# Sixteen of 28 quarter sums of the output weights moved from batch 1 to the end of the first stretch, in a fused cross attention and SwiGLU kernel

## The chip, the cores and the metric

The kernel runs on one core of a Trainium2 chip. The metric is the device time of the whole kernel in microseconds, the median of repeated executions. A profiled execution, recorded separately, gives the traces that are read here; its *span* reaches from the first to the last recorded instruction, and its own device time is a little longer. The engines are written as the profile writes them: PE is TensorE (matrix products), PEld its loads of stationary operands, DVE is VectorE, ACT is ScalarE, POOL is GpSimd, and SP is SyncE, whose queue issues most of the DMA transfers.

## The reference

Two parts follow each other. The first is a block recurrent cross attention: for each of 8 batches and 8 heads, 512 tokens `x` attend to 32 state vectors, and the state vectors attend to the tokens, with 64 elements per head:

```python
scores = scale * np.matmul(x, state.transpose(0, 1, 3, 2))
a = softmax(scores);  xread = np.matmul(a, state)
a2 = softmax(scale * np.matmul(state, x.transpose(0, 1, 3, 2)))
sread = np.matmul(a2, x)
attn = np.concatenate([xread, sread], axis=2)
```

(`softmax` stands for the maximum, exponential and division that the reference writes out.) The heads are joined into rows of 512, 544 rows per batch, 4352 in all. The second part is a feed-forward net on these rows: an RMS norm, two products with weights 512 x 1536 (`w_gate`, `w_val`), `silu(g) * val`, and a product with `w_out`, 1536 x 512. Its weights arrive as 64-bit floats.

## The kernel before, in words

**Stages.** The core works through a first stretch, then batches 1 to 7, then the state rows of all batches together. Each stage is a set of generators, called streams. Each stream yields after a step of one or a few instructions. A string of letters, one letter per step, deals the steps of the streams in order; with the schedule set to manual, that is the order of each engine's instructions. `ORDER` deals the first stretch, `FIRST` batch 1, `PERIOD` batches 2 to 6, `LAST` batch 7 and `STATES` the state rows. An engine executes its own steps in the order in which the letters come; between engines only data and buffers are waited for.

**The first stretch** (404 letters before). It converts the weights: `exponents` (letter e, on ScalarE, lines 234 to 239) and `values` (d, on VectorE, lines 260 to 272) turn each piece of raw 64-bit numbers into 32-bit floats `w_m` (first layer, one tile per pair `mp` of hidden blocks) and `wo` (output weights). It reads the tokens and the states of batches 0 and 1 (a, A and s, S: transposes, scores, softmax; lines 289 to 526, line 289 on GpSimd). It multiplies the first-layer weights of a pair with the states (`own_weights`, v, the product at L567), so that the hidden layer of batch 0 needs only products with the attention weights: letters h (products, L610), t (silu, L616) and u (VectorE's product, L620). The output projection of batch 0 follows as hidden blocks become ready (`project_as_ready`, p, L817), and c copies and stores it. Letter w begins batch 1 (`slot_sums` and its first two pairs of `own_weights`, with `more_of_v`, L594 to L597, on GpSimd). Letter k is `weight_sums` (L860): twelve VectorE instructions that make differences of the halves of the output weights, three tiles t1, t2 and t4 and one difference in place, in three rounds of four, one instruction per step. Letter z, 42 times, is `keep_awake`, a product that nothing uses.

**Batches 1 to 7** compute the hidden layer and the projection with two forms of fast matrix multiplication that save products and cost sums. In `hidden_seven` seven block products (L714, letter h) serve for eight, with ScalarE's copies (t) and VectorE's sums at lines 777 to 802 (u). In `project_twice` seven products of halves (letter p, L1017) are each split once more into seven products of quarters. The left-hand sums are made by VectorE (`quarter_sums` and `half_sums`, L1065 to L1076, letter k), the results are joined by VectorE at L1057 and by GpSimd at L1043 to L1048. Meanwhile the next batch's tokens and states are read (a, s), its `own_weights` made (v, w, x), and SP loads inputs (l), fetches first-layer weights (f, L187) and stores results (o).

**The quarter sums of the output weights.** Each of the seven outer products of `project_twice` needs three sums of quarters of its output weights, and one difference in place. `weight_quarters` (L965 to L974, letter q) makes them once, on GpSimd: seven groups of four instructions at L971, 28 in all. The groups come in the order of `outer_weights`: two blocks of the output weights, then t2, t1, two more blocks (one of them holds the difference in place), t4. After the fourth instruction of a group SP stores its three sums to DRAM (`t2_d`, L973). Every batch, batch 1 too, fetches them back one group at a time (`fetch_quarters`, L963): letters G are the first three fetches of batch 1, letters g always fetch three groups ahead. All these tiles come from one pool of three, `quarters_w`, opened with the other late pools by `open_late` at the first letter c, k or w of the first stretch.

Of the kernel before, what the change touches and what calls it, by code (L numbers as in the profile page):

```python
# [19 lines left out]
W_BUFS = 3  # L20

ORDER = (
    "zzzzzzzzzzazadaaaaaaaaazzzdzzzzzzeaeeaaaaadaadeeaaaaeeezdeazdzzzzzzadeeeaadaadzz"
    "zzzzzzzaaaaaddadzzzzvvvaaedzaAAdaaassdAAAAaAAeeAaAhtddddehehhuppedddddvtduppeeee"
    "ddvvdddeeeedAAddhhtuhhpeAddeApAtddeesvuvddveApdddhheedtupddeeehtAAAddhueeeddsApA"
    "AAdpepvvevAsddddedddphtsssseeehuhAdtssddpdshuedeedpvvvAeApdeAehtdhhAueddppAdddtA"
    "eeddpAheuSSAAAeAAvAvvpehhtSSddhdAAASSpAtuSShSSSdkAuwwsSSSpcpcskpwckkkkkkkkpwkkwc"
    "wwww"
)

PERIOD = (
# [4 lines left out]
)  # L36

FIRST = (
    "vhththhhthfhhuuuhtttuqqqqaxxaaauhthhhvquuhuxqxxaavtuhhththhfaxthhhqqquuuuxxtuhut"
    "hthhthhuaakaavfuuxhtuuhutthqqfhhutxxuqqqqqqhauthuuxhhaautthaaasshtuuhuuthuGhskuk"  # L40
    "GuGukkppqqpppqpppugqqpkkkklkppqpppkcpcqgaakppgqqkskaakaaaaqqppkkpppkppkkpkpkpkpa"
    "cosaaaacgpapgaskkkkkkaosaapppppgcppppcaappaskkakkapppkpapkappaakpookkoosaassfsww"
    "xssswxlscxxcoxofxg"
)
LAST = (
    "vxhhffththhtuhhhavuttuuhhtfuhhgxxthhhuuuxxtuthuhtthuhuxhutuvxxxvhthhutkxghhtuhut"
# [11 lines left out]
def kernel(  # L58
# [791 lines left out]
    def weight_sums():  # L850

        t1, t2, t4 = (seven["t"][:, i] for i in range(3))
        for k in range(0, HM, 2):
            def blk(i, j):
                return wo[:, HM * i + k:HM * i + k + 2, HD * j:HD * j + HD]
            for dst, a, b in ((t1[:, k:k + 2], blk(0, 1), blk(0, 0)),
                              (t2[:, k:k + 2], blk(1, 1), t1[:, k:k + 2]),
                              (blk(0, 1), blk(1, 1), blk(0, 1)),
                              (t4[:, k:k + 2], blk(1, 0), t2[:, k:k + 2])):
                VE.tensor_tensor(out=dst, in0=a, in1=b, op=ALU.subtract)  # L860
                yield
# [272 lines left out]
    done = object()  # L1134
# [18 lines left out]
    def first_of_batch(b):  # L1153
        slot_sums(b)
        yield
        for mp in range(2):
            for part in own_weights(b, mp):
                yield from part
# [12 lines left out]
    for k in range(1, RAW_AHEAD):  # L1171
# [5 lines left out]
               "v": (step for mp in range(NM // 2) for part in own_weights(0, mp) for step in part),  # L1177
               "h": of_batch_0(0), "t": of_batch_0(1), "u": of_batch_0(2),
               "p": project_as_ready(banks_0), "c": projected(banks_0, store_tokens(0)),
               "w": first_of_batch(1), "k": weight_sums(), "z": keep_awake()}  # L1180
    by_hand = dict(engines={mybir.EngineType.PE, mybir.EngineType.DVE,
                            mybir.EngineType.Activation, mybir.EngineType.Pool,
                            mybir.EngineType.SP})
    with tc.manual_schedule(**by_hand):
        for stream in ORDER:
            if stream in "ckw" and "s" not in seven:
                early.close()
                open_late()
            next(streams[stream])
        assert all(next(stream, done) is done for name, stream in streams.items() if name != "z")  # L1190

        for b in range(1, B):
            h, t, u = hidden_seven(S, weights_of(b), lambda b=b: tokens_of(b), True)
            p, c, k, o = project_twice(b, store_tokens(b))
            own = [own_weights(b, mp) for mp in range(2, NM // 2)]
            then = [own_weights(b + 1, mp) for mp in range(2)] if b + 1 < B else []
            streams = {"h": h, "t": t, "u": u, "p": p, "c": c, "k": k,
                       "v": (step for part in own for step in part[0]),
                       "x": (step for part in own + then for step in part[1])}
            streams.update(o=o, f=fetches(b), g=fetches_of_quarters(b))  # L1200
            if b == 1:
                streams.update(q=weight_quarters(), G=first_fetches_of_quarters())
            if b + 1 < B:
                streams.update(l=loads(b + 2) if b + 2 < B else iter((0, 0)), a=tokens_read(b + 1), s=states_read(b + 1),
                               w=first_products(b + 1, then))
            else:
                streams["a"] = (step for part in (state_norm(), sums_of_w([0])) for step in part)
            for stream in FIRST if b == 1 else LAST if b + 1 == B else PERIOD:
                next(streams[stream])
            assert all(next(stream, done) is done for stream in streams.values())  # L1210
        n = B * (NM // 2)
        h, t, u = hidden_seven(NT, (state_weights, state_sums), state_tokens, True,
                               lambda mp: fetch(n + mp + W_BUFS))
        p, c, k = project_seven(NT, store_states, nc.scalar)
        list(weights_back())
        streams = {"h": h, "t": t, "u": u, "p": p, "c": c, "k": k, "y": sums_of_w(range(1, NM // 2))}
        for stream in STATES:
            next(streams[stream])
        assert all(next(stream, done) is done for stream in streams.values())
# [29 lines left out]
```

## Time and profile before

Three executions took 764.33, 761.76 and 761.35 us: the median is 761.76 us.

| what | value |
|---|---|
| median | 761.76 us |
| profiled execution, own time | 762.78 us |
| its span | 760.5 us |
| instructions | 14354 |
| TensorE busy | 747.2 us, 98% |
| VectorE busy | 600.3 us, 79% |
| ScalarE busy | 351.1 us, 46% |
| GpSimd busy | 294.0 us, 39% |
| first stretch, to the last product L567 | 135.78 us |
| batch 1 | 87.64 us |
| batches 2 and 3 | 80.19 and 80.16 us |
| quarter sums L971 in batch 1 | 28, 31.48 us of GpSimd |

The busy time of an engine counts its recorded instructions, and an average over the span mixes stages with different limits; so the borders of the stages were taken from the timeline of TensorE (the last product of each stage), and busy times read between them. A line of a group or of the timeline names the source line, the engine, the operation, the written tile `<-` the read tiles, the shape, and how many instructions are meant; what stands in brackets is the idle time before it and what ended it. "Pair 5" below is the last pair of hidden blocks. In the timeline one product of the code is two records.

### The profile page before, as it was taken

Reading aid. Unit: us, or ns where it says so; the run is one execution under the profiler, and the core shown is the slowest. Engines: PE = TensorE matmul, PEld = TensorE weight load, DVE = VectorE, ACT = ScalarE, POOL = GpSimd, SP = SyncE. Lnnn points to the kernel's source line nnn. Section 1 sums busy time; section 2 is a strip of 40 time slices with the busy share of each in tenths; the row PEclk is TensorE's granted clock in tenths of the full one; section 3 lists DMA queues with packets and bytes.
Section 4 is the critical chain, followed back from the end, with each engine's and each line's share of the span. In section 5 each row is a group of like instructions: output and inputs, shape, how many; then the busy total and the mean of one; then the engine's idle time right before and its main releaser. Section 6 shows DMA issues by size and latency. Waiting matters only on the chain.

```text
span 760.5 us, 14354 instructions
## 1 busy us (share of the span) xinstructions
PE 747.2 (98%) x5608; PEld 595.3 (78%) x5608; DVE 600.3 (79%) x1000; ACT 351.1 (46%) x548; POOL 294.0 (39%) x379
## 2 busy tenths in 40 slices
PE   8899999999899999999999999999999999999998
PEld 6534435678778798879877997889788987899997
DVE  3999997679956898589947994799579975787961
ACT  4898974553225532654155424553355236411220
POOL 2000002893675325542374038312843266323700
PEclk9999999999999999999999999999999999999999
DMA  9787754695576266834774376617662756133411
GB/s 291 214 277 264 289 214 162 231 305 178 195 234 242 56 244 214 297 78 181 256 245 151 125 267 219 222 40 306 217 228 39 293 184 241 56 90 119 140 56 28
DMA packets 61890, 146.15 MB, mean 192 GB/s; under 512 B 15744, under 2 KB 32640, under 8 KB 54912
## 3 DMA queue, kind: packets, MB, share of 16 engines
q1 hardware_dynamic: 48704, 125.78, 47.3%
q10 hardware_dynamic: 13120, 19.47, 9.0%
q8 instruction: 44, 0.72, 0.4%
q14 instruction: 22, 0.18, 0.1%
HBM read 116.46 MB, written 28.77 MB: 191 GB/s over the span
## 4 chain that ended last, share of the span: by engine, by line
PE 88%; DVE 8%; POOL 1%; ACT 1%; issue 1%; DMA 0%; SPq 0%; ACTq 0%; POOLq 0%; DVEq 0%
PE f L714 36%; PE f L1017 27%; PE f L817 6%; PE pv L610 5%; PE at L567 3%; PE pv L567 2%; PE f L880 2%; PE at L345 1%; PE f L1149 1%; PE at L509 1%; PE at L440 1%; DVE hb L1076 1%; DMA out_dram<-kept 0%; PE at L296 0%; DVE hb L790 0%
## 5 line engine op out<-in xcount | busy, mean ns | idle before, releaser
L714 PE MATMUL f<-aT_s,v 128*128 128x256 f32 x504 | 119.6, 382 | 0.0
L714 PEld LDWEIGHTS f<-aT_s,v 128*128 128x128 f32 x504 | 94.5, 190 | 24.8 <-issue 9.2
L777 DVE TENSOR_TENSOR g<-g,f 128x512 f32<-128x512 f32 x84 | 57.3, 685 | 42.6 <-PE f L714 38.6
L1043 POOL TENSOR_TENSOR kept<-kept 128x256 f32<-128x256 f32 x28 | 23.1, 826 | 175.0 <-DVE kept L1057 173.6
L714 PE MATMUL f<-aT_t,vs 128*128 128x256 f32 x336 | 87.2, 383 | 0.3 <-ACT g L761 0.3
L1027 ACT COPY kept<-f 128x512 f32<-128x512 f32 (+1 forms) x56 | 29.7, 532 | 124.8 <-PE f L1017 83.0
L1017 PE MATMUL f<-w,h 128*128 128x128 f32 x588 | 74.6, 276 | 1.0 <-DVE h L1067 1.0
L714 PEld LDWEIGHTS f<-aT_t,vs 128*128 128x128 f32 x336 | 62.4, 190 | 16.0 <-POOL vs L594 4.2
L1017 PEld LDWEIGHTS f<-w,h 128*128 128x128 f32 x588 | 69.6, 192 | 5.4 <-issue 4.1
L768 ACT ACTIVATE hb<-g 128x1024 f32<-128x1024 f32 x42 | 44.5, 1058 | 56.7 <-DVE g L777 56.6
L594 POOL TENSOR_TENSOR vs<-v 128x256 f32<-128x256 f32 x42 | 31.7, 755 | 80.4 <-ACT v L579 80.4
L289 POOL TENSOR_TENSOR ri<-ss,mhalf 128x4 f32<-128x4 f32 x8 | 10.4, 1295 | 124.5 <-DVE ss L371 114.6
L766 ACT COPY g<-f 128x512 f32<-128x512 f32 x42 | 24.6, 586 | 44.5 <-PE f L714 44.5
L714 PE MATMUL f<-aT_t,v 128*128 128x256 f32 x168 | 43.5, 381 | 1.6 <-DVE c L777 1.6
L817 PE MATMUL f<-wo,hb 128*128 128x512 f32 x96 | 44.4, 600 | 0.0
L610 PE MATMUL pv<-aT_s,v 128*128 128x512 f32 x96 | 43.7, 597 | 0.3 <-ACT t L616 0.3
L714 PE MATMUL f<-aT_s,vs 128*128 128x256 f32 x168 | 43.6, 382 | 0.0
L790 DVE TENSOR_TENSOR hb<-hb,c 128x512 f32<-128x512 f32 (+1 forms) x48 | 36.9, 768 | 8.0 <-ACT hb L768 7.3
L790 DVE TENSOR_TENSOR hb<-hb,f 128x512 f32<-128x512 f32 (+1 forms) x48 | 31.0, 646 | 15.0 <-PE f L714 15.0
L1017 PE MATMUL f<-wo,h 128*128 128x128 f32 x336 | 42.2, 275 | 0.0
L1017 PE MATMUL f<-wo,hb 128*128 128x128 f32 x336 | 42.1, 275 | 0.0
L777 DVE TENSOR_TENSOR c<-c,f 128x512 f32<-128x512 f32 (+1 forms) x48 | 31.2, 650 | 12.6 <-PE f L714 12.5
(183 smaller groups left out, 1689.1 us busy)
## 6 DMA issues: line engine op xcount, KB each, us to landing
w_m<-w_d SPq DMA_DIRECT2D x48, 1024.0 KB, 5.9
w<-t_d SPq DMA_DIRECT2D x49, 576.0 KB, 5.4
out_dram<-kept SPq DMA_DIRECT2D x56, 128.0 KB, 2.1
raw<-in_moe_w_val_dram SPq DMA_DIRECT2D x6, 1024.0 KB, 5.5
raw<-in_moe_w_out_dram SPq DMA_DIRECT2D x6, 1024.0 KB, 7.1
w_d<-w_m SPq DMA_DIRECT2D x6, 1024.0 KB, 4.9
x_b<-in_x_dram SPq DMA_DIRECT2D x6, 1024.0 KB, 7.5
x_d<-xB ACTq DMA_DIRECT2D x6, 1024.0 KB, 4.2
```

Of the source, the lines that this page charges most:

```text
L567: TE.matmul(out=pv[e][Ns * j:Ns * j + Ns, :], lhsT=stT_g[b][D * e:D * e + D, j, :], rhs=w[D * e:D * e + D, j].rearrange("p m k f -> p (m k ...
L594: GE.tensor_tensor(out=vs[:, 0], in0=a21, in1=a22, op=ALU.add)
L610: TE.matmul(out=to[0], lhsT=lhs(i, k), rhs=r, start=(i == 0), stop=(i == len(rhs) - 1))
L714: TE.matmul(out=ps[:, i, 0:half], lhsT=l[:, i, :], rhs=r, start=(start and i == 0 and k == 0), stop=(k == len(lhs) - 1), skip_group_check= ...
L766: SE.copy(gates(q)[1], q["x"][:, :, 0:half])
L768: SE.activation(out=hb[:, 2 * mp:2 * mp + 2, 0:n].rearrange("p m (c t) -> p m c t", c=2), in_=q["g"][:, :, :, 0:half], func=ACTF.Silu if s ...
L777: VE.tensor_tensor(out=to, in0=to, in1=q[ps][:, :, 0:half], op=ALU.add)
L790: VE.tensor_tensor(out=part, in0=part, in1=val, op=ALU.mult)
L817: TE.matmul(out=banks[r], lhsT=hb[:, m, P * r:P * r + P], rhs=wo[:, m, :], start=(m == 0), stop=(m == NM - 1))
L1017: TE.matmul(out=to[half][:, slot, :], lhsT=lhs[:, k, :], rhs=rhs[:, k, :], start=(fresh and n in (0, 4) and k == 0), stop=(k == QM - 1), s ...
L1027: SE.copy(k[:, 4 * i:4 * i + 4 - i], banks[name][i])
L1043: GE.tensor_tensor(out=k[:, 1:3], in0=k[:, 0:1].to_broadcast([P, 2, QD]), in1=k[:, 1:3], op=ALU.add)
```

## The change

Sixteen letters q are added to `ORDER`, among its last letters, which then has 420; `FIRST` has 12 in place of 28, and 322 letters in place of 338. The generator `weight_quarters` is made with the first stretch's streams and handed on to batch 1. All other letters occur as often as before in each string, and in another order. The other four stages' strings are the same. From line 1181 on the line numbers of the kernel after are higher by one.

```diff
--- before.py
+++ after.py
@@ -20,12 +20,12 @@
 W_BUFS = 3
 
 ORDER = (
-    "zzzzzzzzzzazadaaaaaaaaazzzdzzzzzzeaeeaaaaadaadeeaaaaeeezdeazdzzzzzzadeeeaadaadzz"
-    "zzzzzzzaaaaaddadzzzzvvvaaedzaAAdaaassdAAAAaAAeeAaAhtddddehehhuppedddddvtduppeeee"
-    "ddvvdddeeeedAAddhhtuhhpeAddeApAtddeesvuvddveApdddhheedtupddeeehtAAAddhueeeddsApA"
-    "AAdpepvvevAsddddedddphtsssseeehuhAdtssddpdshuedeedpvvvAeApdeAehtdhhAueddppAdddtA"
-    "eeddpAheuSSAAAeAAvAvvpehhtSSddhdAAASSpAtuSShSSSdkAuwwsSSSpcpcskpwckkkkkkkkpwkkwc"
-    "wwww"
+    "zzzzzzzzzzaazdaaaaaaaaadeeaazzezzzzzzzzzzzzzzazzaaaaadadzzzzaaazzeeeeedadzadaadz"
+    "zadaaazzeeeedzdzaaaadvAaavdadaAAaavessaAAAeAeAAdahhhhteeeddddddtuppdddvdAAeeeupv"
+    "ddvhhhheeeeddAdtAAeddpdeAupteedsddvedAddeepvvhhheeeAddtupdAeetAeepdAdduppdAAdAdv"
+    "vhdvhAdeAduheeddAsssddAsdppsdtuhedeeedApdtdAedAsedhuddvpvvhhethssduepeeedtseAApp"
+    "AAAddddAddAveeepvhddsvAAdhhhhkAqsuASttSSSqkukqkkqquAAwpqSSSSwSwwwwwkkpkSSSpcqpkp"
+    "SSkckkqqqqcpcqqqqwwq"
 )
 
 PERIOD = (
@@ -36,11 +36,11 @@
 )
 
 FIRST = (
-    "vhththhhthfhhuuuhtttuqqqqaxxaaauhthhhvquuhuxqxxaavtuhhththhfaxthhhqqquuuuxxtuhut"
-    "hthhthhuaakaavfuuxhtuuhutthqqfhhutxxuqqqqqqhauthuuxhhaautthaaasshtuuhuuthuGhskuk"
-    "GuGukkppqqpppqpppugqqpkkkklkppqpppkcpcqgaakppgqqkskaakaaaaqqppkkpppkppkkpkpkpkpa"
-    "cosaaaacgpapgaskkkkkkaosaapppppgcppppcaappaskkakkapppkpapkappaakpookkoosaassfsww"
-    "xssswxlscxxcoxofxg"
+    "qhhtaahGtathhuvvhhulhxxttfaatuhhtaaxxxuuxhuqqqqhhuuththhhththaaaahuuhuuuhtttffGh"
+    "uuhtvxxxqkkvxkkhuhuhuxaathtahutuhhtahhuuxuuthhtuhthhtaahhuauGuuuuhpptaaqfugaaupa"
+    "hqpuuuppgqkkkkckkakpqappgkkkcppppkppkkkkakkkssspppcpppcpppppcpppppaakassaaosskkk"
+    "aokaaaaackakkpkqapppkppppppppqgkpakgoossaalkssaakkksoosppcsaapwwwxxxxxppcfgxoofs"
+    "sg"
 )
 LAST = (
     "vxhhffththhtuhhhavuttuuhhtfuhhgxxthhhuuuxxtuthuhtthuhuxhutuvxxxvhthhutkxghhtuhut"
@@ -1177,7 +1177,8 @@
                "v": (step for mp in range(NM // 2) for part in own_weights(0, mp) for step in part),
                "h": of_batch_0(0), "t": of_batch_0(1), "u": of_batch_0(2),
                "p": project_as_ready(banks_0), "c": projected(banks_0, store_tokens(0)),
-               "w": first_of_batch(1), "k": weight_sums(), "z": keep_awake()}
+               "w": first_of_batch(1), "k": weight_sums(), "q": weight_quarters(), "z": keep_awake()}
+    quarters_made = streams["q"]
     by_hand = dict(engines={mybir.EngineType.PE, mybir.EngineType.DVE,
                             mybir.EngineType.Activation, mybir.EngineType.Pool,
                             mybir.EngineType.SP})
@@ -1187,7 +1188,7 @@
                 early.close()
                 open_late()
             next(streams[stream])
-        assert all(next(stream, done) is done for name, stream in streams.items() if name != "z")
+        assert all(next(stream, done) is done for name, stream in streams.items() if name not in "qz")
 
         for b in range(1, B):
             h, t, u = hidden_seven(S, weights_of(b), lambda b=b: tokens_of(b), True)
@@ -1199,7 +1200,7 @@
                        "x": (step for part in own + then for step in part[1])}
             streams.update(o=o, f=fetches(b), g=fetches_of_quarters(b))
             if b == 1:
-                streams.update(q=weight_quarters(), G=first_fetches_of_quarters())
+                streams.update(q=quarters_made, G=first_fetches_of_quarters())
             if b + 1 < B:
                 streams.update(l=loads(b + 2) if b + 2 < B else iter((0, 0)), a=tokens_read(b + 1), s=states_read(b + 1),
                                w=first_products(b + 1, then))
```

## The prediction

> **What bounds the kernel now.** I read the busy shares first, then the busy time by stage, then the waits of TensorE in each stage, then the timelines of VectorE and GpSimd side by side.
>
> ```profile
> PE 747.2 (98%) x5608; PEld 595.3 (78%) x5608; DVE 600.3 (79%) x1000; ACT 351.1 (46%) x548; POOL 294.0 (39%) x379
> ```
>
> TensorE (PE) sets the time; only 13.3 of its 760.5 us are idle, so a gain can come only from idle or stretched TensorE time. The table by stage says where that is (borders at the last product of each stage; columns: length, then busy time and instructions of each engine):
>
> ```profile
> core 0: us, PE busy (x) PEld busy (x) DVE busy (x) ACT busy (x) POOL busy (x), PEclk, DMA share, GB/s
> 0.00:40.31 40.31, 35.60 (x187) 24.62 (x187) 28.51 (x46) 26.90 (x37) 6.00 (x28) 1.00 0.87 249
> 40.31:112.96 72.65, 72.65 (x329) 29.59 (x329) 69.64 (x87) 63.22 (x74) 0.00 (x0) 1.00 0.73 260
> 112.96:135.78 22.82, 22.82 (x166) 11.16 (x166) 18.56 (x32) 11.79 (x19) 5.16 (x7) 1.00 0.56 201
> 135.78:223.42 87.64, 83.27 (x671) 68.20 (x663) 71.19 (x116) 33.13 (x56) 61.99 (x67) 1.00 0.67 219
> 223.42:303.61 80.19, 80.19 (x670) 68.21 (x662) 64.44 (x115) 35.54 (x59) 35.54 (x47) 1.00 0.57 197
> ```
>
> The first stretch ends at 135.78. Batch 1 takes 87.64, batch 2, with the same products, 80.19 (batch 3: 80.16): batch 1 has 7.45 us too many, 4.37 of them idle TensorE. It differs by GpSimd's 28 quarter sums (L971, 31.48 us) and 6.8 us more busy VectorE (DVE) for one more instruction. TensorE's waits in batch 1; batch 2 shows none:
>
> ```profile
> PE f L714 <- DVE c L777: 1.6, 1, 1.6
> PE at L440 <- DVE aT_s L433: 1.0, 1, 1.0
> PE f L1017 <- DVE h L1067: 1.0, 1, 1.0
> PE at L524 <- DVE sr L520: 0.7, 1, 0.7
> ```
>
> All four name VectorE. The timelines (start, duration) say why; the second and fourth line are GpSimd's at the same moments:
>
> ```profile
> 143.35 1.21 DVE L790 TENSOR_TENSOR hb<-hb,c 128x512 f32<-128x512 f32 x1 [0.26 <-ACT hb L768]
> ...
> 143.97 1.45 POOL L971 TENSOR_TENSOR wo<-wo 128x384 f32<-128x384 f32 x1
> ...
> 193.37 2.93 DVE L1076 TENSOR_TENSOR hb<-hb 128x768 f32<-128x768 f32 x2
> ...
> 193.77 1.72 POOL L971 TENSOR_TENSOR wo<-wo 128x384 f32<-128x384 f32 x1
> ```
>
> L790 takes 0.69 elsewhere, L1076 0.95 each, L971 1.01 alone: on overlap both stretch. Divided over all, 6.8/28 = 0.24 us of VectorE per quarter sum.
>
> [...] L790 and L1076 (two SBUF inputs) are stretched by 0.5 to 0.8 us, L777 (one input in PSUM) keeps 672 to 689 ns throughout.[...]
>
> **The change, part by part.** No arithmetic is added or removed. 16 of 28 letters q move from batch 1's string into the last part of the first stretch's, and both strings are dealt anew, which permutes products, copies and sums of these two stages on every engine.[...] I worked from the built order of each engine, with durations from the trace of before (for queued instructions the spacing of starts).
>
> *1. The first stretch gets longer.* Up to the conversion that starts at 36.14 both orders hold equal VectorE work. From there before's VectorE is the near-critical engine: 69.64 of 72.65 us busy. Its last piece of the weights of pair 5, which a TensorE product (L567) needs, ends at 111.2:
>
> ```profile
> 109.97 1.22 DVE L272 SCALAR_TENSOR_TENSOR w_m<-raw,ex 128x1024 f32<-128x1024 f32 x1
> ...
> 111.94 1.09 PE L567 MATMUL at<-w_m,stT_g 64*32 64x512 f32 x16
> ```
>
> These 75 us hold about 2 us of VectorE waits (1.0 on L239, 0.7 on L610, the rest at single places), so 73.0 of work. After's order has the same plus one L450 (0.61) ahead of those weights: 36.14 + 73.0 + 0.61 = 109.75 without any wait; with the 0.25 us that such a release takes, the product starts at 110.0, or at 110.7 if 0.7 of the waits stay. TensorE's own work would let it start at about 108.3. It takes 1.0. Behind it after's TensorE has 28 records of L817 (0.43 each, 0.1 per switch: 12.53), 20 of L610 (8.69), two stages of L567 (1.90), L509 (1.13), L483 (0.97), L367 (0.81), L296 (0.43) and L524 (0.38): 26.84 us, against 22.82 behind it in before. So the stage ends at 111.0 to 111.7 + 26.84 = 137.9 to 138.6, and small waits in that tail can add to it: a second L610 behind the L620 of its bank (0.7 of 1.0 not covered at worst). I take 138.4: **+2.6 us** (137.9 to 139.3: +2.1 to +3.5). ScalarE has two more table loads here, at 1.28 us each in the trace[...]; it is idle 9.4 of the 72.65 us, so I count them as hidden behind the lateness of VectorE; without that cover, each adds up to 1.28, and the upper bound holds most of one.
>
> *2. Not all 16 sums leave batch 1.* The third group of sums (w2 of t2) needs the last VectorE sums of output weights (L860). Those stand behind the last L520 and L526, which wait for TensorE near the stage's end, so they end at about 138. Only some 9 quarter sums can run before; some 19 overlap batch 1 rather than 12.
>
> *3. Batch 1 gets shorter.* Its new order on TensorE and VectorE is nearly that of batch 2, so its floor is 80.2, and the four waits above go. What remains is 19 sums at 0.24 = 4.6 us of stretched VectorE. In batch 2 VectorE has 15.7 us idle, but none after 26 us of the hidden half, where the last L777 has no margin against its product; the second half has margins of about 0.4 us. Before's excess of 7.45 for 28 sums would scale to 5.1 for 19; with the order that fits, I take a third of that, 1.6 (0.3 to 4): batch 1 = 81.8, **−5.8 us** (−7.1 to −3.5).
>
> *4. The transfers.* Each group of sums is stored by SP (L973) and fetched back into a pool of three tiles (`quarters_w`, L963). SP's queue takes them in order: in after the first store stands ahead of two fetches of weights and of the tokens' load. That store waits for GpSimd's fourth sum, which is ready at about 120, so the fetches behind it keep their time; L328 needs the tokens at about 140 and gets them at 137 to 139. In batch 1 slots two to five are each refilled only when TensorE has read the slot before, about 7.4 us ahead of need; landing takes (minimum 3.3, median 5.4, maximum 7.7). [...] Cost nothing, covered by the other products of L1017; without the cover 0.3 us each.
>
> The four sums L594 of more products (pair 1 of batch 1) stand behind nine quarter sums on GpSimd: done about 7.5 us into batch 1, needed at 8.0. Cost nothing, with little margin.
>
> **Sum.** +2.6 − 5.8 = −3.2; span 760.5 → 757.3. The profiled execution took 762.78, 2.28 outside its span, and it stands 1.02 above the median of 761.76. So 762.78 − 3.2 = 759.6 for that execution, and 758.6 against the median.
>
> **Rivals.**
>
> B, *the gain in full.* VectorE's small waits in the first stretch are gone and TensorE is not held at pair 5 (+0.5 to +1.5), and batch 1 nears 80.5 to 81: −5 to −7.4, so 754.3 to 757. For it: waits of VectorE are small already and the new order may have none. Against: 73 us of conversion stand before that product in any order.
>
> C, *the late sums keep batch 1 slow.* If 19 sums cost nearly what they cost in before (5.1; 4 where idle VectorE absorbs some) and the stretch grows by 3, the sum is 3 − 7.45 + 4 = −0.4; with 3.5 and 5.1 it is +1.2: 761 to 763, or 764 with a wait of ScalarE. For it: L777 has no margin. Against: three of the four waits shown stand at single places of an order that is gone.
>
> D, *slower: the ring of slots becomes the bound.* The place is L963 in batch 1's second half. If landings under the load of batch 1 take 10 us in place of 5.4, each of five refills holds L1017 for 10 − 7.4 = 2.6, 13 in all: 761.8 − 3.2 + 13 = 771.6. It breaks even where the five stalls sum to 3.2 (8.0 us per landing) and is slower by 0.5% from 8.8. For it: a maximum of 7.7, and DMA busy at 0.67 in batch 1. Against: the median.
>
> That the sums do not move at all is excluded by the built order; that few of them move is part of C.
>
> **Chances.** The stated case (both effects, 756.5 to 760.5, centre 758.6) 0.49; B 0.20; C 0.17; D 0.14. About 0.5% (3.8 us) is what a measurement here can tell from no change: faster is below 757.95, slower above 765.57. Faster: B whole and a third of the stated case, 0.36; slower: D; within: the rest, 0.50. The range leaves out a little of B below (754.6) and D above (764.5).
>
> **What would show it.** Right: the product L567 of pair 5 starts near 110.5 behind a VectorE release, the first stretch ends at 138 to 139, nine or so L971 stand before that, batch 1 takes 81 to 83 us, batches 2 to 7 stay at 80.2. Step 1 is wrong if the stretch ends before 137; step 3 if TensorE still waits for VectorE for over 3 us in batch 1; step 4 if L1017 or L973 is seen waiting for a DMA. A stage outside these two that changes by over 0.5 us would make the whole sum wrong.

## The result, and the profile after

The changed kernel took 766.16 us (median of five executions; one of them, the one whose profile was kept, ran at a mean clock of 0.557 and took 1287.63; it is used for nothing here). The kernel before took 762.21 beside it. The ratio of the comparable executions (after over before) is 1.0049, with a 95% interval of 1.0027 to 1.0071. Measured again with the first experiments it was 1.0064 (1.0040 to 1.0088). The forecast was 758.6, so the change moved the time the other way.

The profile shown here is that of a second profiled execution of the same kernel: its own time is 766.68, its span 764.9, against 760.5 before. The busy shares of its page hardly differ from those of before:

```profile
PE 748.2 (98%) x5608; PEld 598.4 (78%) x5608; DVE 598.8 (78%) x1000; ACT 353.6 (46%) x550; POOL 292.2 (38%) x379
```

The table by stage tells more. It is cut where the first product of the next stage's string starts, which is where the borders of before lie too (length, then busy time and instructions of each engine):

```profile
core 0: us, PE busy (x) PEld busy (x) DVE busy (x) ACT busy (x) POOL busy (x), PEclk, DMA share, GB/s
0.00:139.11 139.11, 133.24 (x673) 67.81 (x673) 117.49 (x162) 103.00 (x130) 24.16 (x47) 0.98 0.74 247
139.11:227.04 87.93, 82.35 (x664) 68.76 (x662) 68.55 (x115) 35.37 (x60) 47.93 (x56) 1.00 0.66 215
227.04:307.20 80.16, 80.16 (x663) 68.23 (x670) 64.76 (x116) 34.55 (x57) 34.81 (x46) 1.00 0.56 191
```

The first stretch ends at 139.11 in place of 135.78, **+3.33** (forecast +2.6, bounds +2.1 to +3.5). Batch 1 takes 87.93 in place of 87.64, **+0.29** (forecast −5.8). What follows takes 537.86 in place of 537.08, +0.78. The sum is +4.40. So the loss in the stretch came about as large as forecast, and the gain in batch 1 did not come at all. Two more things stand in the table: the mean clock of the first stretch is 0.98 where it was 1.00, and batch 1 is still far from the 80.16 of batch 2.

The +0.78 does not lie in the batches that follow: batches 2 to 7 are alike, but for batch 4 of the kernel before, which was 0.57 longer than its neighbours. It lies behind the last product, where ScalarE issues the last two stores (the kernel before first, the changed one second; start, duration):

```profile
757.47 0.85 ACTq L1132 DMA_DIRECT2D out_dram<-h  x2
760.50 2.33 ACTq L1132 DMA_DIRECT2D out_dram<-h  x2
```

From the end of the last product to the end of the span it is 3.44 us before and 4.83 after. Over the 17 traces looked at here this end takes 3.4 to 3.5 us in twelve and 4.7 to 4.9 in five, with old and new orders among them, so these 1.4 us of the two spans' difference of 4.4 are not shown to come from the change.

Here are the last weights of pair 5 and their product in the changed kernel, from the timelines of VectorE and TensorE. In the kernel before the product began later, at 111.94, but with 4 us less of TensorE's work behind it:

```profile
110.17 1.22 DVE L272 SCALAR_TENSOR_TENSOR w_m<-raw,ex 128x1024 f32<-128x1024 f32 x1
...
111.53 1.21 PE L567 MATMUL at<-w_m,stT_g 64*32 64x512 f32 x16
```

The waits of TensorE in batch 1 of the changed kernel:

```profile
engine line waited for: us in total, times, longest us
PE at L509 <- DMA e<-e_d: 1.8, 1, 1.8
PE f L714 <- ACT g L761: 1.6, 1, 1.6
PE at L345 <- DMA xG<-x_d: 1.3, 1, 1.3
PE f L1017 <- DVE h L1067: 0.7, 1, 0.7
PE f L1017 <- DVE hb L790: 0.2, 1, 0.2
```

Of the 4.3 us for which TensorE waited for VectorE before, 0.9 are left: that part of the forecast came true. In their place stand two waits for transfers and one for ScalarE. ScalarE's own timeline shows that the wait for ScalarE comes from a transfer as well (start, duration, what it did, in brackets the idle time before it):

```profile
156.32 0.59 ACT L766 COPY g<-f 128x512 f32<-128x512 f32 x1 [1.14 <-PE f L714]
159.00 2.35 ACTq L335 DMA_DIRECT2D xG<-x_d  x4
161.39 1.06 ACT L768 ACTIVATE hb<-g 128x1024 f32<-128x1024 f32 x1 [4.49 <-issue]
```

ScalarE issues the transfers that bring the next batch's tokens into their transposed form: one store to DRAM (L330, `x_d<-xB`) and four fetches back (L335, `xG<-x_d`). A fetch reads what the store has written, so it is issued when the store has landed. The store was issued at 150.33. The chain that ended last, taken for this part, tells the rest (start, duration):

```profile
150.33 8.64 DMA x_d<-xB
158.98 0.02 issue
159.00 0.35 ACTq L335
...
160.81 10.20 DMA xG<-x_d
171.01 0.09 issue
171.10 1.09 PE at L345 x14
```

The store takes 8.64 us, and until it lands, at 158.97, ScalarE's queue stands at the fetch, which is issued at 159.00. Together with the 2.35 us of the four issues themselves, ScalarE's compute is idle for 4.49 us ahead of the silu of the hidden layer (L768). With the same four fetches issued in batch 1 of the kernel before, that idle time was 2.40, so some 2.1 us of it are extra. The copy behind the silu (L761) comes late, and TensorE's L714 waits 1.6 us for it. Then the last fetch takes 10.20 and holds L345. In batch 2 of the same execution the same store and fetches land in 3.1 to 5.3 us, and nothing waits. The silu, which stands behind the four fetches in ScalarE's order, began at 161.39, 0.04 us after their issues had ended (161.35).

### The profile page after: what moved, and what is told of

It reads as the page before. It is cut to its first block, busy times and chain, and to the rows that moved or that the text cites. A ratio compares the mean times of both kernels' runs of the same rounds, so it can differ in the third digit from the quotient of the medians.

```text
span 1285.8 us, 14363 instructions
## 1 busy us (share of the span) xinstructions
PE 1276.3 (99%) x5608; PEld 855.2 (67%) x5608; DVE 602.6 (47%) x1000; ACT 357.5 (28%) x550; POOL 280.9 (22%) x379
## 4 chain that ended last, share of the span: by engine, by line
PE 96%; issue 3%; POOL 0%; ACT 0%; POOLq 0%
PE f L714 40%; PE f L1017 31%; PE f L817 6%; PE pv L610 6%; PE at L567 3%; PE pv L567 3%; PE f L880 3%; PE at L509 1%; PE at L345 1%; PE at L440 1%; PE at L296 1%; PE at L483 0%; PE at L318 0%; PE at L537 0%; POOL groups L159 0%
## 5 line engine op out<-in xcount | busy, mean ns | idle before, releaser
L714 PE MATMUL f<-aT_s,v 128*128 128x256 f32 x504 | 205.9, 582 | 0.0
L714 PEld LDWEIGHTS f<-aT_s,v 128*128 128x128 f32 x504 | 110.8, 222 | 97.2 <-issue 65.9
L714 PE MATMUL f<-aT_t,vs 128*128 128x256 f32 x336 | 146.4, 582 | 0.0
L1017 PEld LDWEIGHTS f<-w,h 128*128 128x128 f32 x588 | 117.5, 299 | 8.7 <-issue 8.5
L1017 PE MATMUL f<-w,h 128*128 128x128 f32 x588 | 122.9, 389 | 0.0
L714 PEld LDWEIGHTS f<-aT_t,vs 128*128 128x128 f32 x336 | 76.6, 229 | 55.9 <-issue 22.8
L594 POOL TENSOR_TENSOR vs<-v 128x256 f32<-128x256 f32 x42 | 31.0, 737 | 245.7 <-ACT v L579 245.7
L790 DVE TENSOR_TENSOR hb<-hb,f 128x512 f32<-128x512 f32 (+1 forms) x48 | 31.4, 654 | 108.7 <-PE f L714 108.7
L817 PE MATMUL f<-wo,hb 128*128 128x512 f32 x96 | 76.7, 965 | 0.0
L610 PE MATMUL pv<-aT_s,v 128*128 128x512 f32 x96 | 75.8, 968 | 0.0
L768 ACT ACTIVATE hb<-g 128x1024 f32<-128x1024 f32 x42 | 44.4, 1057 | 109.3 <-DVE g L777 109.3
L714 PE MATMUL f<-aT_s,vs 128*128 128x256 f32 x168 | 73.3, 578 | 0.0
L714 PE MATMUL f<-aT_t,v 128*128 128x256 f32 x168 | 72.4, 588 | 0.0
L1017 PE MATMUL f<-wo,h 128*128 128x128 f32 x336 | 70.7, 391 | 0.0
L1017 PE MATMUL f<-wo,hb 128*128 128x128 f32 x336 | 69.9, 389 | 0.0
L1017 PEld LDWEIGHTS f<-wo,hb 128*128 128x128 f32 x336 | 67.4, 288 | 2.2 <-issue 0.4
L1017 PEld LDWEIGHTS f<-wo,h 128*128 128x128 f32 x336 | 68.4, 305 | 0.0
L714 PEld LDWEIGHTS f<-aT_s,vs 128*128 128x128 f32 x168 | 37.8, 228 | 31.5 <-issue 20.4
L1017 PE MATMUL f<-w,hb 128*128 128x128 f32 x252 | 56.8, 387 | 0.0
```

The lines of the kernel that those rows point to most:

```text
L594: GE.tensor_tensor(out=vs[:, 0], in0=a21, in1=a22, op=ALU.add)
L610: TE.matmul(out=to[0], lhsT=lhs(i, k), rhs=r, start=(i == 0), stop=(i == len(rhs) - 1))
L714: TE.matmul(out=ps[:, i, 0:half], lhsT=l[:, i, :], rhs=r, start=(start and i == 0 and k == 0), stop=(k == len(lhs) - 1), skip_group_check= ...
L768: SE.activation(out=hb[:, 2 * mp:2 * mp + 2, 0:n].rearrange("p m (c t) -> p m c t", c=2), in_=q["g"][:, :, :, 0:half], func=ACTF.Silu if s ...
L790: VE.tensor_tensor(out=part, in0=part, in1=val, op=ALU.mult)
L817: TE.matmul(out=banks[r], lhsT=hb[:, m, P * r:P * r + P], rhs=wo[:, m, :], start=(m == 0), stop=(m == NM - 1))
```

## The experiments

**Each half of the change alone.** The first run, `a_again`, is the changed kernel itself. Three further kernels combine old and new orders.

> The changed kernel once more, for a trace at the clock of the timed runs. Theory 1 (the new order of the first stretch costs the time, and TensorE's granted clock falls in it for some microseconds: the timed runs show a mean of 0.993 to 0.996 where before shows 1.000, which is 2.5 to 5 us at half clock): the first stretch ends at 140 to 144, batch 1 takes 81 to 84, later stages as in before. Theory 2 (the quarter sums still slow batch 1): the stretch ends at 138 to 139 and batch 1 takes 86 to 88 us. Theory 3 (the loss lies outside the two stages): batches 2 to 7 differ from 80.2 us.

Measured: the stretch ends at 139.11, batch 1 takes 87.93, and the batches that follow are as before. That is what theory 2 gave in numbers, though the waits above are not collisions of VectorE and GpSimd (the stretching on overlap: 1.21 us of L790 in place of 0.69). Theory 1 had the clock right (0.994) and batch 1 wrong, and for theory 3 nothing is left: the 0.78 us stand behind the last product.

The second, `move_alone`, keeps the old orders and moves only the letters:

```diff
 ORDER (its end)
-ckkkkkkkkpwkkwcwwww
+ckkkkkkqqqqqqqqkkpwkkwcwwwwqqqqqqqq
 FIRST: its first 16 letters q are taken out
```

> The orders of before, with only the 16 steps moved: 8 behind the last sums of weights of the first stretch that they need, 8 at its end; the first 16 steps q are gone from batch 1's string, and nothing else is dealt anew. Theory 1 (the new order of the first stretch is what costs): this kernel has the old order there, so the stretch ends at 135.8 to 137, the clock stays at 1.000, batch 1 is shorter by 1 to 4 us, and the time is 758 to 761. Theory 2 (the sums slow batch 1 wherever in it they are): batch 1 stays at 86 to 88 and the time at 761 to 764. My forecast's share of a quarter us per sum that leaves batch 1 gives 759 to 760.

> The changed kernel's first stretch with batch 1 as in before, less its first 16 steps q. Theory 1: the stretch ends as in the changed kernel (140 to 144), the clock is below 1.000 as there, batch 1 is 83 to 86, and the time 765 to 769: slower than before. Theory 2: the stretch ends at 138 to 139, and the time is 762 to 765.

> The first stretch of before with the 16 steps added at its end, and the changed kernel's batch 1. Theory 1: the stretch ends at 135.8 to 137, the clock stays at 1.000, batch 1 takes 81 to 84, and the time is 755 to 759: faster than before. Theory 2: batch 1 takes 86 to 88 us here too, and the time is 761 to 764.

(`new_first_stretch` has the changed `ORDER` with the `FIRST` of `move_alone`, `new_batch1` the `ORDER` of `move_alone` with the changed `FIRST`.)

Measured: `new_first_stretch` 765.29 (ratio 1.0040, 1.0025 to 1.0055), stretch to 139.03, batch 1 87.2, clock 0.996: the new stretch alone makes the kernel slower. Its batch 1 has the old order with 12 sums in place of 28, and yet it is only 0.4 us shorter than the 87.64 of before, and TensorE's four waits for VectorE are still there:

```profile
PE f L714 <- DVE c L777: 1.0, 1, 1.0
PE at L440 <- DVE aT_s L433: 1.0, 1, 1.0
PE f L1017 <- DVE h L1067: 1.0, 1, 1.0
PE at L524 <- DVE sr L520: 0.7, 1, 0.7
```

So in the old order the 16 sums were not what held batch 1. The other two are no clean answers. `move_alone` took 773.5 (1.0154), `new_batch1` 770.23 (1.0121); in both the stretch ended where it did before (135.4 and 135.6) at a clock of 1.00, and batch 1 took 99.7 and 95.6. The place that I gave the first eight sums was bad: in GpSimd's order L594, which early products of batch 1 need, stood behind them. In both kernels the clock fell in batch 1 as well (means of 0.95 and 0.98 there). The waits of TensorE in batch 1 of `move_alone`:

```profile
PE at L345 <- DMA xG<-x_d: 3.6, 1, 3.6
PE f L714 <- POOL vs L594: 3.6, 1, 3.6
PE at L440 <- DVE aT_s L433: 1.0, 1, 1.0
```

In these kernels the place of the sums among GpSimd's other work counts for more than their number. And the wait for the tokens is here too, in an order of batch 1 that is the old one, less some sums.

**What holds the new batch 1: transfers or collisions?** Two kernels take away one each.

```diff
 FIRST (part): the four fetches, L345 and what follows later
-ththaaaahuuhuuuhtttffGhuuhtvxxxqkkvxkkhuhuhuxaathtahutuhhtahhuuxuuthhtuhthht
+ththhuuhuuuhtttffGhuuhaaaatvxxxqkkvxkkhuhuhuxththutuhhthhauuxuuthahatuhathht
```

> The changed kernel with one edit in batch 1's order: the four fetches of the next batch's tokens from DRAM (L335) and the products with them (L345) stand later, where the orders of batch 2 and of batch 1 before have them (fetches after 24 steps h in place of 19, products after 33 in place of 27). Theory R (in batch 1 the tokens' way through DRAM takes 8.6 and 9.4 us in place of 4.2 and 4.4 in batch 2, because it meets the stores and fetches of weights; ScalarE's queue stands for 4.5 us at the fetch, and TensorE waits at L714 and L345): both waits go or shrink below 0.5 us, batch 1 takes 83 to 85 us in place of 87.9, and the time is 761 to 764. Theory C (VectorE's collisions with the 19 late sums hold batch 1): it stays at 87 to 88 us and the time at 765 to 768.

```diff
                              (w2[:, 2], b21, w2[:, 1]), (b12, b22, b12)):
-                GE.tensor_tensor(out=to, in0=a, in1=b, op=ALU.subtract)
-                if to is b12:
+                if to is not b12:
+                    GE.memset(to, 0.0)
+                else:
                     nc.sync.dma_start(out=t2_d[o], in_=w2)
```

> The changed kernel with the arithmetic of all quarter sums left out: GpSimd fills the three tiles of a group with zeros instead and the difference in place is not made; stores, fetches and all orders are the same. The output weights' sums, and so the results, are not those of the reference. Theory R: the traffic is the same, the two waits for the tokens' way remain, batch 1 shortens by 0 to 2 us (86 to 88), the time is 764 to 767. Theory C: VectorE is free of collisions, batch 1 takes 81 to 84 us and the time is 759 to 762. My forecast put the sums' share at 1.6 us.

Measured: `tokens_later` takes 85.63 in batch 1 (profiled span 762.1), the wait of L714 is gone, and that of L345 is 0.8. Its median of 765.89 (ratio 1.0069, 1.0042 to 1.0095) is not told apart from the changed kernel's, so theory R's time did not come true. `no_sums`, which leaves the arithmetic of the sums out, takes 84.22 in batch 1 and 762.67 in all (1.0003, 0.9982 to 1.0025), about 4 us under the changed kernel. That is more than theory R allowed and just outside what theory C gave (81 to 84, 759 to 762). It does not separate them cleanly, since without the sums the wait of L345 was gone as well, and the one of L509 was 0.6 in place of 1.8, while L714 still waited 1.4 us for ScalarE. So the sums have a part in the loss that these runs do not separate from the transfers'. VectorE's busy time in batch 1 fell from 68.55 to 66.35 without the sums.

**Which traffic?** One kernel moves a single fetch of 1 MB out of the way of the tokens.

```diff
 FIRST (part): one letter f later
-xxttfaatuhhtaaxxxuuxhuqqqqhhuuththhhth
+xxttaatuhhtaaxxxuuxhuqqqqhhuuththfhhth
```

> The changed kernel with one fetch of first-layer weights (1 MB, L187, issued at 148.8 us just ahead of the tokens' store to DRAM) moved from behind 8 steps h of batch 1 to behind 15. Theory R: the tokens' store (L330) then meets less traffic: it lands in 4 to 6 us in place of 8.3 to 8.7, ScalarE's queue stands for under 2 us at the fetches behind it (4.5 before), and the wait of L714 for ScalarE (1.4 to 1.6 us) shrinks below 0.5; batch 1 loses 1 to 4 us of its 87.9 to 92.7. If the traffic of that fetch has no part in it, the store still takes over 8 us and the wait stays.

The tokens' transfers in batch 1 of this kernel, with the times from issue to landing of the store and the four fetches:

```profile
L335 ACTq DMA_DIRECT2D xG<-x_d x4: 352/443/444, 156.1 to 157.5; - x4
L330 ACTq DMA_DIRECT2D x_d<-xB x1: 377/377/377, 150.0 to 150.0; - x1
...
DMA to landing us min/median/max: 3.3/4.6/5.8
```

The store was issued at nearly the same time (150.0), and store and fetches land in 3.3 to 5.8 us, as in batch 2. Both waits for the tokens are gone. So it was this one fetch that the store met. The four fetches, issued 2.9 us earlier for it, had landed by 163.3 at the latest (the last was issued at 157.5, and none took over 5.8). In batch 1 of the kernel before a fetch of the same size was issued 3.1 us ahead of the store, in place of 1.5, and the store (L330) took half as long from issue to landing:

```profile
L330 ACTq DMA_DIRECT2D x_d<-xB x1: 376/376/376, 152.8 to 152.8; - x1
...
DMA to landing us min/median/max: 4.3/4.3/4.3
```

But the time is 767.99 (1.0058), and batch 1 takes 89.5: the weights now come too late, and L567 waits 3.9 us for them. The mechanism of the two waits is shown; this remedy only moved the wait.

Two more kernels free the tokens' way in other ways, and put L509 later. The first is `tokens_later` with one more edit:

```diff
 FIRST (end)
-ssaakkksoosppcsaapwwwxxxxxppcfg
+ssaakkksooppcaapswwwxxxxxpspcfg
```

> The kernel with the tokens' fetch later, and with the products L509 of the state's read two to three steps p later too, as in batch 2's order (L509 waited 1.8 to 2.6 us for its operand's way through DRAM in all runs of the new batch 1 but one). Theory R: both waits of TensorE for a DMA are below 0.5 us, the clock stays at 1.00 in batch 1, which takes 82 to 85 us; the time is 759 to 763, and its runs spread less (within 3 us). Otherwise it stays at 85.6 us or more.

```diff
 FIRST (start): transposes, store and fetches of the tokens earlier (L509, later in the string, as in the run before)
-qhhtaahGtathhuvvhhulhxxttfaatuhhtaaxxxuuxhuqqqqhhuuththhhththaaaahuuhuuu
+qhhtaahaGtthahauvvhaahulhxxttftuhhtxxxuuxhuqqqqhhaaaauuththhhththhuuhuuu
```

> The changed kernel with the tokens' transposes, store and fetch all earlier in batch 1 (store after 6 steps h in place of 10, fetches after 13 in place of 19), ahead of the weights' fetches, products L345 where the change has them, and L509 two to three steps p later. Theory R: the tokens are there when L345 wants them, ScalarE's queue stands for under 2 us, and batch 1 takes 82 to 85 us. If VectorE's collisions were the cause, four more of its instructions ahead of the sums would make batch 1 no shorter than 86.

Measured: in `both_later` batch 1 takes 83.66 and no wait for a transfer is left in it, but L714 waits 2.3 us for ScalarE in batch 2, which takes 82.64 in place of 80.2. Its executions spread from 761.64 to 770.37, not within 3 us, with a median of 766.42 (1.0041, 1.0025 to 1.0057): the expectation of the profile came true, that of the time did not. `earlier` takes 84.30 in batch 1, and 81.60 in batch 2, where L714 waits 1.3 us; it takes 763.62 in all, 1.0004 (0.9990 to 1.0019). That is about 2.5 us under the changed kernel's first result and level with before, in spite of its longer first stretch. Issuing the transfers earlier was worth more here than using them later; the traces, which differ by 1.1 us in span, do not show why the medians differ by 2.8.

**The clock, and the first stretch.** In the changed kernel TensorE's granted clock falls near 32 us. Here are both kernels over the same times, the changed one first (stretch, length, TensorE busy, clock, DMA share, GB/s):

```profile
30.00:32.00 2.00, 1.35 (x9) 1.00 1.07 315
32.00:34.00 2.00, 1.35 (x8) 0.67 0.87 303
34.00:36.00 2.00, 1.36 (x7) 0.50 0.64 262
36.00:38.00 2.00, 1.96 (x9) 0.50 0.02 1
38.00:40.00 2.00, 2.00 (x5) 0.62 0.84 251
40.00:42.00 2.00, 2.00 (x6) 1.00 0.70 272
```

```profile
30.00:32.00 2.00, 1.77 (x16) 1.00 1.11 373
32.00:34.00 2.00, 1.55 (x14) 1.00 0.91 283
34.00:36.00 2.00, 1.32 (x11) 1.00 0.80 328
36.00:38.00 2.00, 2.00 (x8) 1.00 0.00 0
```

The idle times of TensorE here are up to 0.71 us each; the clock is at half for 6.8 us. The changed kernel begins with L817 1.69 us later than before (45.53 against 43.84). The first of two runs adds unused products where the clock falls, the second moves one instruction of VectorE away from ahead of the last weights:

```diff
 ORDER (part): five letters z more
-dvAaavdadaAA
+dvzzAaazvdazdazAA
```

> The changed kernel with five more products that nothing uses (z), between 28 and 36 us, where the new order has TensorE idle and its granted clock falls to half until 40 us. Theory K (the fall of the clock delays the first stretch, which TensorE bounds): the clock stays at 1.00, the stretch ends at 136.5 to 138 in place of 139.1, and the time is 1 to 2.5 us shorter, 764 to 766. My forecast's step 1 (VectorE's conversion of the last weights holds the product of pair 5): the clock may stay up, but the stretch still ends at 138.5 to 139.5, and the time stays at 766 to 768.

```diff
 ORDER (part)
-ddddAddA
+dddddAdA
```

> The changed kernel with one instruction of VectorE (L450, 0.61 us) moved from ahead of the last converted weights of pair 5 to behind them. My step 1: the product of pair 5 starts 0.6 us earlier (110.9) and the stretch ends 0.6 us earlier, at 138.5. Theory K: TensorE is itself not ready before 111.4, so start and end stay within 0.2 us of 111.5 and 139.1. The time differs by less than can be told either way: the profile decides.

Measured: `awake` kept the clock at 1.00 from 20 to 45 us, but its stretch ended at 138.81, only 0.30 earlier, as step 1 would have it; the five products and a new wait of L610 (0.6) may have taken the place of the fall. Its batch 1, the same order, took 91.29 in that execution, with a wait of 2.51 us at L345 after which the clock was at half for 3.4 us. Its median is 766.12, 1.0030 (1.0010 to 1.0050): slower than before, and not told apart from the changed kernel. `squares_later` (766.67, 1.0041, 1.0002 to 1.0081) had the weights of pair 5 at 110.92 in place of 111.39, and their product still began at 111.50 (111.53 in the changed kernel): TensorE itself was not ready, as theory K said. Batch 1, the same order again, took 92.69 there, with the wait of L345 at 2.5 and the clock lower (0.96); so the 87.93 shown above is not the most that this order takes.

So the lateness of TensorE arises earlier. The next kernels take their start from the old order; the second of them also has the batch 1 of `earlier`:

```diff
-ORDER = (the changed kernel's)
+ORDER = (the first 173 letters of the one before, then those
+         letters of the changed one that remain, in its order)
```

> The changed kernel with the order of before up to the eleventh step A of the first stretch (the product L345 of batch 1's tokens, at about 52 us), then the steps that remain in the changed kernel's order. Theory E (the loss arises before 52 us, where TensorE waits for ScalarE's copies of tokens and products and its clock falls): the clock stays at 1.00 before 60 us, the stretch ends at 135.8 to 136.8, and the time is 2 to 3.5 us below the changed kernel's. Forecast's step 1 or any cause after 52 us: the stretch ends at 138.5 to 139.5 as in the changed kernel.

> The same first stretch with the batch 1 of the run earlier (tokens' way through DRAM earlier, L509 later). If both causes are right and add up: the stretch ends at 135.8 to 136.8, batch 1 takes 83 to 85 us, and the time is 758 to 761, under that of before by 1.5 to 4 us. If batch 1 takes back what the stretch gives (its transfers start earlier by the clock, and meet others), batch 1 takes 86 or more and the time is that of before.

Measured: `old_start` 764.21 (1.0011, 0.9991 to 1.0031), `old_start_earlier` 761.93 (0.9999, 0.9984 to 1.0014). In the profiled executions of both the clock fell anyway, from 34.8 to 41.6 us, in the very order in which it had stayed up in the kernel before, and the stretches ended at 141.1 and 141.3. That is not what I expected, and it answered something else: the old order falls in some executions and not in others. Of the 150 executions of the kernel before that ran beside all experiments, 118 have a mean clock of 0.999 or more, with a median span of 760.1; in 32 it is 0.994 to 0.996, with a median span of 762.8. So a lower clock goes with **2.7 us** more; where it fell in these executions is not recorded. All eight comparable executions of the changed kernel have a mean of 0.993 to 0.996. The seven of 20 executions of `old_start` at 0.999 or more have a median span of 757.5, about what was forecast; but these are the best of a kernel with another order, picked by their clock, and no proof of the forecast.

The traces say more on this chance. In all 17 of them every stretch between two changes of the clock, from its first rise on, is a whole multiple of 3.413 us. The first rise came 4.9 to 7.7 us after the first instruction (in the kernel before at 6.09, where the time of one record of L1149 goes from 634 to 379 ns), and the fall, in the 11 traces that have it, eight such steps later. Here are steps seven and eight behind the rise, and the one after, first in the kernel before (rise at 6.09), then in `old_start` (rise at 7.47), whose order is the same up to there (stretch, length, TensorE busy, clock, DMA share, GB/s):

```profile
26.57:29.99 3.42, 2.86 (x24) 1.00 0.40 156
29.99:33.40 3.41, 3.18 (x27) 1.00 1.00 312
33.40:36.81 3.41, 2.29 (x15) 1.00 0.66 264
```

```profile
27.95:31.37 3.42, 2.86 (x24) 1.00 0.38 150
31.37:34.78 3.41, 2.72 (x20) 1.00 0.99 311
34.78:38.19 3.41, 2.73 (x13) 0.50 0.45 184
```

In the 11 traces with the fall TensorE was busy for 0.60 to 0.80 of step eight, in the six without it for 0.93 or more, behind a step seven of 0.81 to 0.84 in all. A single step of 0.67 between fuller ones, as the last of the kernel before, was followed by no fall. So the same order may fall or not by where these steps happen to lie. That is my reading of these traces; that it is what makes one in five of the kernel before fall was not tested.

The last pair tests whether unused products keep the clock up; `kept_start` has the tokens' way of `earlier` too, with L509 where the change has it.

```diff
 ORDER (part): three letters z more, in the old order
-edzaAAdaaassdAAAAaAAeeAaA
+edzaAAdzaaassdzAAAAzaAAeeAaA
```

> The kernel before with three more products that nothing uses (z) between 31 and 37 us, nothing else. If short idle times of TensorE there let the clock fall in a fifth of its executions: nine in ten executions at 0.999 or above, and a span of 760 to 761 in these. If the fall doesn't hang on TensorE's idle time there: one execution in five still at 0.994 to 0.996, as before.

> The run old_start with the same three unused products, and with the tokens' way through DRAM earlier in batch 1 (L509 where the change has it). If the clock's falls and the tokens' way together were the loss: clock 0.999 or above in most executions, spans of 757 to 760, and a median of 759 to 762, 1 to 3 us below that of before. If something else of the new order holds it, the clock stays up and the spans are 760 or more.

Measured: `before_awake` 762.3 (0.9998, 0.9988 to 1.0008), eleven of twelve executions at 0.999 or more (28 of 35 of the kernel before, beside it). By counts alone this is a hint, no proof. `kept_start` takes **760.69, ratio 0.9978 (0.9967 to 0.9989)**, with 19 of 22 executions at 0.999 or more; it is a little faster than the kernel before, and so than the changed one. Its table by stage, and then its longest waits in batch 1:

```profile
0.00:137.55 137.55, 132.30 (x678) 66.06 (x679) 117.27 (x162) 103.06 (x130) 24.18 (x47) 1.00 0.75 250
137.55:221.19 83.64, 80.79 (x664) 68.54 (x662) 67.64 (x115) 35.34 (x60) 48.47 (x56) 1.00 0.70 227
```

```profile
PE at L509 <- DMA e<-e_d: 1.1, 1, 1.1
PE f L714 <- ACT g L761: 0.9, 1, 0.9
```

With the clock up the stretch ends 1.77 us later than before and batch 1 is 4.0 shorter; the span is 757.9. Here the product of pair 5 begins at 109.97, right behind the weights:

```profile
108.61 1.22 DVE L272 SCALAR_TENSOR_TENSOR w_m<-raw,ex 128x1024 f32<-128x1024 f32 x1
...
109.97 0.78 PE L567 MATMUL at<-w_m,stT_g 64*32 64x512 f32 x8
```

One attempt to do better, with the first stretch of before whole, eight sums at its end and 20 in batch 1, was slower:

```diff
 ORDER (the one of before)
-wkkwcwwww
+wkkwcwwwwqqqqqqqq
 FIRST of both_later: 20 letters q in place of 12, from the eighth letter h on,
 and one letter G later
```

> An attempt to beat both: the first stretch of before, with only 8 of the steps q at its very end behind all that batch 1 begins with, and the batch 1 of the run both_later with 20 steps q spread over it. If steps 1 and 3 of the forecast and theory R are right together: the stretch ends at 135.6 us and the clock stays at 1.00 in it, no wait for a DMA over 0.5 us, batch 1 takes 83 to 86 us, and the time is 756 to 760. If sums in the hidden half cost more than the 0.24 us each that the forecast used, batch 1 takes 87 or more and the time is 761 or more.

Measured: 772.17 (1.0110). Batch 1 takes 95.8 us: TensorE waits 5.1 us for a copy of ScalarE and 2.3 for L594 in it, and its mean clock is 0.95. The stretch ended at 138.9 with the clock fallen (0.50 from 35 to 40 us).

## Why the prediction was wrong, point by point

**Step 1, the first stretch gets longer by 2.6: held in size, with a term missing.** It was 3.33. The mechanism that was argued (73 us of conversion and one L450 ahead of pair 5's weights) fits `kept_start`, which starts in the old order with the clock up: it has the product at 109.97 where 110.0 was worked out, and the end at 137.55 against 137.9. (The release itself took 0.14 us there, where 0.25 was taken.) In the changed kernel itself the product began at 111.53, since TensorE and with it VectorE were late: "TensorE's own work would let it start at about 108.3" was wrong there, for it was ready at 111.5. The 1.56 us between 3.33 and 1.77 go with the new order's start, in which the clock fell. The fall alone does not account for them: in `awake`, with that start, five more products and the clock up, the product began at 111.23 and the stretch ended at 138.81.

**Step 2, some 19 sums overlap batch 1: right.** GpSimd's groups show 19 instructions of L971 in batch 1.

**Step 3, batch 1 gets shorter by 5.8: its parts held, its sum did not.** The floor is right (80.16). VectorE was busy for 3.8 us more than in batch 2, 0.20 per sum where 0.24 was taken. TensorE's waits for VectorE fell to 0.9 us. But "what remains is 19 sums" was not true. Of the 7.77 us by which batch 1 is longer than batch 2, 4.7 are the waits of step 4 and 0.9 those for VectorE; the other 2.2 stand in TensorE's busy time (82.35 against 80.16), and no wait names their cause. These last two make 3.1 us where 1.6 (0.3 to 4) was taken for the sums. And VectorE's time per sum is no price for the batch: `new_first_stretch` has 16 sums less in the old order and gained 0.4 us, where 16 x 0.24 = 3.8 would be expected.

**Step 4, the transfers cost nothing: this is the step that failed.** It put nothing where the trace has 4.7 us. It followed only the quarter sums' own transfers and the load of the tokens, and found them hidden, as they were: no L1017 waited for a fetch. It did not ask for the transfers that ScalarE issues, and so put their cost at nothing, though the new order has them elsewhere: the store of the next batch's tokens after 10 steps of products in place of 19, its fetches after 19 in place of 28, L345 after 27 in place of 34. The distances did not shrink (nine steps from store to fetch in both, eight in place of six from fetch to L345); what changed is the company. Store and fetches took 4.2 and 3.1 to 5.3 us in batch 2, and I took the orders' likeness to batch 2 for likeness in time; in batch 1 the store met a fetch of 1 MB issued 1.5 us ahead of it, which batch 2 does not have at that point, and took 8.64, and the last fetch took 10.20. The three waits on transfers, direct or over ScalarE, sum to 4.7 us in that execution; 1.8 of them are L509's, whose transfer is the state's and was not looked into.

**The clock was in no step.** The table of the kernel before shows 1.00 in all stages, and I took it as given. If a fall costs the changed kernel what a lower clock goes with in the kernel before, and since 118 of 150 executions of that one have none, it is an estimated 2.7 x 118/150 = 2.1 us of the 3.95 (766.16 − 762.21). `awake`, the direct test, neither shows nor excludes that: its ratio of 1.0030 lies below the changed kernel's 1.0049 and 1.0064, with intervals that overlap.

**The rivals.** C (late sums) went up to 764, two short of the result, for a reason that is at most a part of it. D alone had the result in its range, and named transfers in batch 1 as the way to a slower kernel, but at the wrong place: the ring of slots never held TensorE. That D covered the result is luck, since the transfers that it followed were not the ones that held TensorE.

## What to carry to other kernels

When an order is dealt anew, list every chain that leaves the core and comes back, on whatever queue it is issued, with the distance in work from issue to use in both orders, and with what else is under way at that time: the distance that sufficed beside nothing (4.2 us) did not beside another megabyte (8.64). Where the issue of a transfer waits for another transfer, look at what stands behind it on the issuing engine; here it was ScalarE's silu, with 4.49 us of idle time ahead of it. And read TensorE's clock per stage over several executions, not in one profile: the kernel before lost none in its profile, and had a lower clock in 32 of 150 executions.

## What the runs showed of the hardware that had not been expected

The clock fell with no idle time of TensorE over 0.8 us nearby: TensorE was 68% busy from 30 to 36 us in the changed kernel, with a longest idle time of 0.71 us, and in `old_start`, whose order there is the old one, 86% from 30 to 35 us, with a longest of 0.56 us ahead of the fall at 34.78. In the kernel before the clock was lower in about one execution of five (32 of 150). In the 17 traces the clock is 0.50 or 1.00, with mixed values only where a stretch holds both, and it changed in whole multiples of 3.413 us. The fall lasted 6.8 us in the first stretch, and 3.4 us behind the wait of 2.51 us at L345 in `awake`, so that this wait cost more than its own length: the first three groups of four records of L714 behind it took 4.38 us, and the next two groups 0.87 and 0.86 us each.
